# Transposing u by DMA instead of on TensorE, from the third batch on

## The chip, the cores and the metric

One core of one Trainium2 chip runs the whole program. The metric is device time in microseconds (us) of that core. A single core has no second die to compare with. A run's device time is about 2 us longer than the span of its trace.

Short names: PE is TensorE doing matmuls, PEld TensorE loading weights (it overlaps PE), DVE VectorE, ACT ScalarE, POOL GpSimd, SP SyncE; SPq is SyncE's queue of DMA issues. L946 is line 946 of the kernel that was profiled, so the same statement has other line numbers in other versions: ch1 is L988 before and L1008 after, ch2 is L1008 before and L1028 after.

## The reference, cut to what matters

A linear attention with a norm is followed by an MLP block over 8 batches of 576 tokens and 512 features:

```python
kv  = einsum('bhsd,bhse->bhde', k, v)
out = einsum('bhsd,bhde->bhse', q, kv)
x   = out / rms(out) * g_norm                 # then heads are joined: (8, 576, 512)
tok = einsum('ts,bsd->btd', w_tok, alpha1 * x + beta1)
u   = x + lam * tok
a2  = alpha2 * u + beta2
ch  = maximum(a2 @ w_ch1, 0) @ w_ch2          # 512 -> 2048 -> 512
return u + lam * ch
```

`u` is made with tokens on the partitions, and `a2 @ w_ch1` contracts over the features, so u has to be transposed before the first MLP matmul (ch1). alpha2 and beta2 belong to features, so after the transposition they are one value per partition.

## The kernel before

The kernel is a list scheduler written in Python: every operation is entered with its possible engines, an estimated cost on each and the tiles that it reads and writes. The scheduler simulates the engines, picks an engine and a place in program order for each operation, and semaphore waits are then put between the engines. Each engine runs its own list strictly in order.

The part that the change replaces is `ut(b)`, for one batch:

```python
def ut(b, pri):
    nc4 = 5 if b % 2 else 4            # odd batches carry the 64-row tails of two batches
    n = 128 * nc4
    def group(djs):
        t = P.ptile(1)                 # a PSUM bank
        for i, dj in enumerate(djs):
            for c in range(nc4):
                P.op({"PE": 0.056}, lambda e, _, ...: e.transpose(
                    bt(i)[:, 128 * c:128 * c + 128], ub[:, c, 128 * dj:128 * dj + 128], identb[:]),
                    r=[..., ("ub", c)], w=[t], kind="T", keep=1, after=[("a2t", dj)])
        for i, dj in enumerate(djs):
            # ACT: activation(Identity, scale=alpha2 column, bias=beta2 column)
            # DVE: tensor_scalar(mult, add) with the same columns; PSUM -> a2t
            ...
    # one group for each of the four blocks of 128 features
```

ub holds u in bf16, tokens on partitions. a2t holds the scaled transpose, [128, 4, 640] bf16, in a single buffer: it cannot be filled for batch b + 1 before the ch1 matmuls of batch b are done with it. In between lie the ch2 matmuls of batch b and the token mixing of batch b + 1.

## Time and profile before

| quantity | before |
|---|---|
| time, median of 4 runs | 373.49 us (372.63 to 374.49) |
| span of the trace | 371.9 us |
| PE busy | 361.9 us, 97% |
| transposes of u on PE | 144, of which 108 from the third batch on |
| PE idle from 103 to 331 us | none |

The first part of the profile page gives busy time, share of the span and number of instructions of each engine:

```profile
PE 361.9 (97%) x2279; PEld 224.1 (60%) x2279; DVE 224.4 (60%) x393; ACT 176.6 (47%) x304; POOL 119.8 (32%) x113
```

TensorE is the bound. Busy time by stretches shows it again (columns: stretch, its length, then busy time and count on PE, PEld, DVE, ACT and POOL, granted clock, share of the DMA engines, GB/s):

```profile
147.00:169.00 22.00, 22.00 (x132) 12.15 (x130) 11.84 (x21) 4.63 (x8) 5.58 (x4) 1.00 0.24 81
189.00:215.00 26.00, 26.00 (x153) 14.70 (x152) 15.58 (x27) 5.61 (x11) 8.50 (x6) 1.00 0.10 38
```

In the steady part PE has no gap, the clock is full, and from 147 us on the DMA engines are mostly idle, because all inputs have been loaded. From 103 to 131 us their share is still 0.52. Work taken from PE here shortens the run one for one, as long as nothing new makes PE wait.

The transposes, and the instructions that evict them, by source line (duration in ns, minimum/median/maximum):

```profile
L946 PE MATMUL ps<-identb,ub x144: 219/219/233, 31.1 to 319.3; 128*128 128x128 bf16 x144
L954 ACT ACTIVATE a2t<-ps,cols x11: 769/876/884, 78.7 to 320.3; 128x640 bf16<-128x640 bf16 x7, 128x512 bf16<-128x512 bf16 x4
```

The 219 ns are one transpose from end to end. They are pipelined, and the chain that ended last shows what they cost in a row (columns: start, time, what):

```profile
317.36 0.89 PE ps L946 x16
318.26 1.08 PE ps L1008 x5
...
331.00 17.39 PE ps L988 x128
348.38 17.28 PE ps L1008 x80
```

Sixteen transposes take 0.89 us, 56 ns each. The two last lines are the MLP of the last batch: its ch1 starts at 331.00 us. The end of the run, from SyncE's timeline (start, length):

```profile
367.13 1.11 SPq L1028 DMA_DIRECT2D out_dram<-xtl  x2
```

### The profile page before, as it was taken

Reading aid. Unit: us, or ns where it says so; the run is one execution under the profiler, and the core shown is the slowest. Engines: PE = TensorE matmul, PEld = TensorE weight load, DVE = VectorE, ACT = ScalarE, POOL = GpSimd, SP = SyncE. Lnnn points to the kernel's source line nnn. Section 1 sums busy time; section 2 is a strip of 40 time slices with the busy share of each in tenths; the row PEclk is TensorE's granted clock in tenths of the full one; section 3 lists DMA queues with packets and bytes.
Section 4 is the critical chain, followed back from the end, with each engine's and each line's share of the span. In section 5 each row is a group of like instructions: output and inputs, shape, how many; then the busy total and the mean of one; then the engine's idle time right before and its main releaser. Section 6 shows DMA issues by size and latency. Waiting matters only on the chain.

```text
span 371.9 us, 5712 instructions
## 1 busy us (share of the span) xinstructions
PE 361.9 (97%) x2279; PEld 224.1 (60%) x2279; DVE 224.4 (60%) x393; ACT 176.6 (47%) x304; POOL 119.8 (32%) x113
## 2 busy tenths in 40 slices
PE   8999999999999999999999999999999999999993
PEld 2787574678766564558855665557755544557541
DVE  3779579993985786738944682738453794410132
ACT  3778775676864276116821376116621273116300
POOL 3654014530353560045502571046502650130000
PEclk9999999999999999999999999999999999999998
DMA  6999999998658119111000110011000210020021
GB/s 179 365 372 386 289 381 303 375 368 250 204 156 269 59 56 335 35 56 58 0 2 28 58 57 2 0 56 58 2 0 28 86 28 0 31 85 2 0 86 56
DMA packets 47798, 48.01 MB, mean 129 GB/s; under 512 B 14096, under 2 KB 38680, under 8 KB 47772
## 3 DMA queue, kind: packets, MB, share of 16 engines
q1 hardware_dynamic: 47520, 47.47, 38.2%
q8 instruction: 18, 0.29, 0.3%
q10 hardware_dynamic: 252, 0.18, 0.1%
q14 instruction: 8, 0.07, 0.1%
HBM read 38.20 MB, written 9.44 MB: 128 GB/s over the span
## 4 chain that ended last, share of the span: by engine, by line
PE 86%; DMA 6%; DVE 4%; ACT 2%; SPq 1%; issue 0%
PE ps L988 33%; PE ps L1008 31%; PE ps L916 10%; DMA st<-in_v_dram 6%; PE ps L591 4%; PE ps L609 3%; PE ps L946 2%; DVE rt L692 1%; DVE yn L690 1%; PE ps L741 1%; ACT w L422 1%; PE ps L1095 1%; DVE small L679 0%; ACT wt L422 0%; PE ps L814 0%; ACT vr L422 0%
## 5 line engine op out<-in xcount | busy, mean ns | idle before, releaser
L988 PE MATMUL ps<-a2t,w 128*128 128x320 bf16 (+1 forms) x768 | 142.3, 329 | 1.7 <-DVE ht L974 0.7
L1008 PE MATMUL ps<-w,ht 128*128 128x512 bf16 x576 | 139.6, 381 | 0.0
L988 PEld LDWEIGHTS ps<-a2t,w 128*128 128x128 bf16 x768 | 73.3, 98 | 44.3 <-DVE ht L974 1.6
L1008 PEld LDWEIGHTS ps<-w,ht 128*128 128x128 bf16 x576 | 54.8, 98 | 59.2
L973 ACT ACTIVATE ht<-ps 128x640 bf16<-128x640 f32 (+1 forms) x103 | 67.2, 653 | 45.0 <-PE ps L988 44.2
L1021 POOL TENSOR_TENSOR xm<-xm,lc 128x512 f32<-128x512 f32 x28 | 37.4, 1335 | 129.5 <-DVE lc L1016 129.5
L1016 DVE TENSOR_TENSOR lc<-ps,lam_bc 128x512 f32<-128x512 f32 x36 | 24.9, 691 | 66.5 <-PE ps L1008 65.8
L695 POOL TENSOR_TENSOR xm<-yn,g_bc 128x512 f32<-128x512 f32 x28 | 43.2, 1543 | 38.3 <-DVE yn L690 37.2
L677 ACT ACTIVATE sq<-ps 128x512 f32<-128x512 f32 (+1 forms) x35 | 20.5, 593 | 47.9 <-PE ps L591 47.6
L924 DVE TENSOR_TENSOR xm<-ps,xm 128x512 f32<-128x512 f32 x28 | 19.2, 690 | 31.0 <-PE ps L916 29.8
L916 PE MATMUL ps<-rt,wt 128*128 128x512 bf16 x140 | 37.3, 381 | 0.0
L591 PE MATMUL ps<-kvc,qt 128*128 128x128 f32 x112 | 32.6, 386 | 0.0
L591 PE MATMUL ps<-identr,qr 128*128 128x128 f32 x112 | 31.6, 375 | 0.4 <-DVE yn L690 0.4
L609 PE MATMUL ps<-vr,kr 128*128 128x128 f32 (+1 forms) x112 | 30.9, 370 | 0.0
L679 DVE TENSOR_REDUCE small<-sq 128x8 f32<-128x512 f32 (+1 forms) x35 | 23.4, 672 | 7.7 <-ACT sq L677 7.2
L692 DVE TENSOR_TENSOR rt<-yn,ge 128x512 bf16<-128x512 f32 x26 | 25.1, 971 | 0.5
L954 ACT ACTIVATE a2t<-ps,cols 128x640 bf16<-128x640 bf16 (+1 forms) x11 | 8.9, 842 | 32.8 <-PE ps L946 32.8
L690 DVE TENSOR_TENSOR yn<-ps,small 128x512 f32<-128x512 f32 (+1 forms) x35 | 23.9, 685 | 0.7
L591 PEld LDWEIGHTS ps<-kvc,qt 128*128 128x128 f32 x112 | 22.1, 199 | 2.3
L916 PEld LDWEIGHTS ps<-rt,wt 128*128 128x128 bf16 x140 | 13.6, 98 | 15.3
L591 PEld LDWEIGHTS ps<-identr,qr 128*128 128x128 f32 x112 | 22.0, 201 | 1.2 <-DVE yn L690 0.7
L609 PEld LDWEIGHTS ps<-vr,kr 128*128 128x128 f32 x112 | 21.7, 200 | 0.3
(147 smaller groups left out, 386.5 us busy)
## 6 DMA issues: line engine op xcount, KB each, us to landing
st<-in_moe_w_ch_dram SPq DMA_DIRECT2D x8, 1024.0 KB, 10.9
out_dram<-xm SPq DMA_DIRECT2D x32, 256.0 KB, 2.3
st<-in_q_dram SPq DMA_DIRECT2D x7, 1024.0 KB, 6.3
st<-in_k_dram SPq DMA_DIRECT2D x7, 1024.0 KB, 8.5
st<-in_v_dram SPq DMA_DIRECT2D x7, 1024.0 KB, 11.7
ht<-in_moe_w_tok_dram SPq DMA_DIRECT2D x2, 576.0 KB, 8.1
kvft<-in_k_dram SPq DMA_DIRECT2D x8, 128.0 KB, 7.3
kvft<-in_v_dram SPq DMA_DIRECT2D x8, 128.0 KB, 5.4
```

Of the source, the lines that this page charges most:

```text
L591: P.op(F, lambda e, _: e.matmul(t.flat()[:, 128 * pr:128 * pr + 128], a(), m(), start=True, stop=True), r=r, w=[t], kind="F", **kw)
L609: return e.matmul(o, a, m, start=(c == 0), stop=(c == 4))
L679: P.op({"DVE": dve_us(512)}, lambda e, _: e.tensor_reduce(out=small[rows, s4], in_=sq[rows, s2], axis=AX.X, op=ALU.add), r=[("sq", s2)], w ...
L690: P.op({"DVE": dve_us(512)}, lambda e, _: e.tensor_tensor(out=hview(yn[rows, s3, :]), in0=hview(t.flat(rows)), in1=bc, op=ALU.mult), r=[t, ...
L692: P.op({"DVE": dve_us(512), "POOL": pool_us(512)}, lambda e, _: e.tensor_tensor(out=rto, in0=yn[rows, s3, :], in1=ge1[rows, :], op=ALU.mul ...
L695: P.op({"POOL": pool_us(512)}, lambda e, _: e.tensor_tensor(out=hview(x), in0=hview(yn[rows, s3, :]), in1=g_bc[rows, None, :].to_broadcast ...
L916: return e.matmul(t.flat(), wt[:, sc, col:col + 128], rt[:, sc, :] if sc < 4 else rtt[:], start=(sc == 0), stop=(sc == 4))
L973: return e.activation(dst, src(), ACT.Relu)
L988: return e.matmul(o, w1[:, dj, 128 * fj:128 * fj + 128], m, start=(dj == 0), stop=(dj == 3))
L1008: P.op({"PE": 0.216}, lambda e, _: e.matmul(t.flat(), ht[:, fj, 128 * c:128 * c + 128], w2[:, fj, :], start=(fj == 0), stop=(fj == 15)), r ...
L1016: o = P.op({"DVE": dve_us(512)}, lambda e, _: e.tensor_tensor(out=lc[:], in0=t.flat(), in1=lam_bc[:], op=ALU.mult), r=[t, "lam"], w=["lc"] ...
L1021: lambda e, _: e.tensor_tensor(out=x, in0=x, in1=lc[:], op=ALU.add),
```

## The change

The intent is to take the transposes off the bounding engine. From the third batch on, each chunk of 128 tokens of ub goes through a transposing DMA on SyncE's queue straight into a2t, and alpha2 and beta2 are applied in place in SBUF. The scaling is free to run on ACT or DVE; no PSUM is used.

```diff
-                    if ye == e and e != "POOL" and y not in o.raw:
-                        continue
@@ the kernel
+        XB = 2
@@ def ut(b, pri)
+            if b >= XB:
+                before = set(o for dj in range(4) for o in P.readers.get(("a2t", dj), ()))
+                before.update(o for dj in range(4) for o in P.lastw.get(("a2t", dj), ()))
+                for c in range(nc4):
+                    o = P.op({"SP": 0.5}, lambda e, _, c=c: e.dma_start(
+                        a2t[:, :, 128 * c:128 * c + 128], ub[:, c, :], transpose=True),
+                        r=[("ub", c)] if c < 4 else [("ubt", 0), ("ubt", 1)], w=[("a2r", c)],
+                        dma_us=0.6, pri=pri)
+                    o.deps.update(before)
+                for dj in range(4):
+                    ... # in place: a2t = a2t * alpha2 + beta2, on ACT or DVE
+                    P.op({"ACT": act_us(n, 2), "DVE": dve_us(n, 4)}, g,
+                         r=["cols"] + [("a2r", c) for c in range(nc4)], w=[("a2t", dj)],
+                         pri=pri - 5, port=True)
+                return
```

The first hunk makes an engine also wait on itself before it overwrites what it has read.

More of the change, by code (lines that the diff above doesn't have):

```diff
@@ L937, in ut, with g @@
             n = 128 * nc4
+            if b >= XB:
[8 more added lines that the diff above has]
+                for dj in range(4):
+                    def g(e, m, dj=dj):
+                        if m == "ACT":
+                            return e.activation(a2t[:, dj, 0:n], a2t[:, dj, 0:n], ACT.Identity,
+                                                scale=cols[:, dj:dj + 1], bias=cols[:, 4 + dj:5 + dj])
+                        return e.tensor_scalar(out=a2t[:, dj, 0:n], in0=a2t[:, dj, 0:n],
+                                               scalar1=cols[:, dj:dj + 1], scalar2=cols[:, 4 + dj:5 + dj],
+                                               op0=ALU.mult, op1=ALU.add)
+                    P.op({"ACT": act_us(n, 2), "DVE": dve_us(n, 4)}, g,
+                         r=["cols"] + [("a2r", c) for c in range(nc4)], w=[("a2t", dj)],
+                         pri=pri - 5, port=True)
+                return
             def group(djs):
```

## The prediction

> **What bounds the kernel now.** TensorE. The page's first part gives PE 97% of the 371.9 us span (DVE 60%, ACT 47%, POOL 32%). In the busy time by stretches PE has no gap from 103 to 331 us; the granted clock is 1.00. The chain that ended last is 86% PE, the transposes of u (L946) 2.0%. The DMA is full until about 85 us; from 147 us its share is 4 to 24%.
>
> **What the change removes.** From the third batch on, 108 of 144 transposes (three batches of 20, three of 16). One shows as 219 ns, but they are pipelined: 16 of them advance PE by 0.89 us in the chain (317.36 to 318.26), 14 by 0.80 us, so 56 ns each. 108 x 56 ns = 6.0 us, all on the critical path as PE has no gaps there: 373.7 - 6.0 = 367.7 us, 1.6%. Also gone are 24 evictions from PSUM (ACT 876 ns, DVE 545 ns median), worth nothing as neither engine limits.
>
> **What it adds.** 27 transposing DMAs of 128x512 bf16 (128 KB) on SyncE, and 24 in-place scalings in SBUF, mostly on VectorE, estimated at 0.3 to 0.5 us, off the path.
>
> **Does the transpose arrive in time?** a2t has one buffer, so the window lies between the u casts and the next batch's first ch1 matmul. Timeline: the last casts start at 114.8, 154.1, 196.4, 238.4, 279.2, 317.9; ch1 at 130.7, 168.8, 215.1, 253.0, 296.4, 330.8. That leaves 12.5 to 18 us after the last cast, 18 to 24 after the first, less about 1 us as ch1 comes earlier. SyncE only stores after 147 us.
>
> One chunk: plain stores of 128 KB and 256 KB land 2.3 us after issue, issue taking 0.33 to 0.6 us. The Trainium skill, "DMA: Bandwidth & Descriptors", section "Latency and other measured facts", gives 261 GB/s for a DMA transpose: estimate 0.5 us for 128 KB, so landing in about 3 us, all landed 5 us after the last cast, no PE wait. "VectorE: DVE Perf Modes", section "The three transpose paths", gives 1309 ns for 128x128: four per chunk serially would be 5.2 us, and five chunks 26 us from the first cast (149.1 to about 177), a stall of some 8 us in each of three odd batches. I take the first as likelier. No run here shows either yet.
>
> **Other effects.** Same-engine write-after-read orders become semaphore waits. A wait on its own previous result costs DVE about 0.1 us (starts 0.71 instead of 0.61 us apart); few are adjacent. I allow 0.3 us, in the start-up up to 66 us, where the chain runs through DVE. Otherwise the first 110 us should be unchanged. The third batch's DMAs meet loads in flight near 107 to 117 us, with 15 us of slack.
>
> **Prediction.** 368.0 us, 80% range 366.4 to 375. Faster by over 2% (below 366.2): 0.06; within 2%: 0.84; slower by over 2%: 0.10. The removed PE work bounds the gain under 2%.
>
> **What would show it.** L946 falls from 144 to 36. PE stays gapless after 103 us; ch1 waits for neither DVE a2t nor the DMA. Transposes land within 2 to 4 us; SyncE issues each in 0.5 to 2 us. Wrong if PE waits for a2t before each ch1, or landing exceeds 5 us.
>
> **What would make it wrong.** Transposes served serially at 5 us or more per chunk; a SyncE issue of several us; a late DMA blocking VectorE in program order, so that PSUM evictions stall PE; or the re-made list schedule moving other work onto the path.

## More of the kernel before

The scheduler prefers to alternate "F" matmuls (float32r, attention) with others, and at the end SyncE waits for every DMA of the program, one wait for each:

```python
rank = (fresh, (o.kind == "F") == (last_kind == "F"))
...
for o in self.sequence:
    if o.lat is not None:              # o is a DMA
        nc.sync.wait_ge(*val[o.idx])
```

## The result

Ratios here are the mean time of one kernel's runs over that of the other's runs of the same rounds, so they are not quite the ratio of the medians.

| | before | after |
|---|---|---|
| time, median of 4 runs | 373.49 us | 368.49 us (368.14 to 368.84) |
| ratio, 95% interval | | 0.9865 [0.9838, 0.9892] |
| span of the trace | 371.9 us | 366.1 us |
| first ch1 matmul of the second batch | 79.65 us | 79.62 us |
| first ch1 matmul of the last batch | 330.83 us | 323.84 us |
| from the one to the other ("the stretch") | 251.19 us | 244.22 us |
| end of the last DMA issue to the end of the span | 3.6 us | 4.9 us |

The run is 5.0 us shorter, 1.35%, against a predicted 368.0 us. The stretch in the table is useful because it hardly varies: everything in it is bound by PE. (Its lengths are taken from unrounded starts.) It is read from PE's timeline, where the matmul itself starts; the chain above lists the same place 0.17 us later. The start-up before it, bound by loads, moves from run to run (in the profiled runs other than experiment 7 the second batch's ch1 starts at 78.7 to 80.0 us), which is also why the two profiled runs differ by 5.8 us and the medians by 5.0.

The profile after, first part of the page:

```profile
PE 355.1 (97%) x2142; PEld 218.4 (60%) x2171; DVE 223.4 (61%) x394; ACT 175.3 (48%) x301; POOL 121.2 (33%) x115
```

PE is 6.8 us less busy and still 97% of a shorter span; it bounds as before. (The count of matmuls fell by 137 instead of 108 because some records are missing from the trace; the count of weight loads fell by exactly 108.) The instructions that use a2t now:

```profile
L941 SPq DMA_TRANSPOSE a2t<-ub x27: 1188/1224/2206, 112.4 to 312.5; - x27
L951 DVE TENSOR_SCALAR a2t<-a2t,cols x19: 401/434/1359, 125.6 to 316.2; 128x512 bf16<-128x512 bf16 x10, 128x640 bf16<-128x640 bf16 x9
L949 ACT ACTIVATE a2t<-a2t,cols x5: 802/920/921, 123.4 to 315.0; 128x640 bf16<-128x640 bf16 x3, 128x512 bf16<-128x512 bf16 x2
...
DMA to landing us min/median/max: 2.4/2.5/6.7
```

SyncE spends 1.2 us on the issue of a transpose of 128x512, which lands 2.5 us after its start (medians). The third batch's transposes meet loads: from 112.4 to 121.7 us the DMA engines are full, and its four transposes land 6.7, 5.2, 3.2 and 3.0 us after their starts. The last batch in time order, from the timelines of SP, DVE, ACT and PE:

```profile
307.09 6.64 SPq L941 DMA_TRANSPOSE a2t<-ub  x5
314.98 0.92 ACT L949 ACTIVATE a2t<-a2t,cols 128x640 bf16<-128x640 bf16 x1 [9.55 <-DMA a2t<-ub]
314.98 1.64 DVE L951 TENSOR_SCALAR a2t<-a2t,cols 128x640 bf16<-128x640 bf16 x3 [0.60 <-DMA a2t<-ub]
323.84 17.55 PE L1008 MATMUL ps<-a2t,w 128*128 128x320 bf16 x128
```

The scaled transpose is complete at 316.6 us, 7.2 us before ch1 asks for it. In the third to seventh batch this slack is 1.8, 8.2, 13.9, 8.4 and 11.7 us. The third is the tightest: its transposes have landed by 123.4 us, but DVE comes to the scaling in its list only at 125.58 us and is done at 127.58 us:

```profile
125.58 2.00 DVE L951 TENSOR_SCALAR a2t<-a2t,cols 128x512 bf16<-128x512 bf16 x3
129.34 1.68 PE L1008 MATMUL ps<-a2t,w 128*128 128x512 bf16 x7
```

PE's waits from 81 to 362 us hold nothing of a2t:

```profile
PE ps L1008 <- ACT ht L993: 0.4, 1, 0.4
PE ps L1008 <- ACT qt L420: 0.4, 1, 0.4
```

And the end, from SyncE's timeline:

```profile
360.14 1.12 SPq L1048 DMA_DIRECT2D out_dram<-xtl  x2
```

The last issue ends at 361.26 us and the span at 366.1 us. So two sizes differ from the prediction: the stretch shrank by 6.97 us where 6.0 was forecast, and the end grew by 1.2 us, which was not forecast at all.

The theory that the experiments test has four parts. First, the gain is PE time alone. Second, a transpose is worth more than 56 ns because some of them stood next to float32r matmuls. Third, the end grew because SyncE executes 27 more waits there, one after the other. Fourth, the transposes have several us to spare, but only because the DMA engines are idle at that time. The rivals are that the gain comes from the PSUM evictions that ACT and DVE no longer do, that the end grew for another reason, and that the arrival was nearly too late. (The slacks above already limit the fourth part: the third batch's transposes came in time with the DMA engines full, and had 1.8 us to spare, not several.)

### The profile page after: what moved, and what is told of

Its sections match the earlier page's. It is cut to its first block, busy times and chain, and to the rows that moved or that the text cites. A ratio compares the mean times of both kernels' runs of the same rounds, so it can differ in the third digit from the quotient of the medians.

```text
span 366.1 us, 5530 instructions
## 1 busy us (share of the span) xinstructions
PE 355.1 (97%) x2142; PEld 218.4 (60%) x2171; DVE 223.4 (61%) x394; ACT 175.3 (48%) x301; POOL 121.2 (33%) x115
## 4 chain that ended last, share of the span: by engine, by line
PE 90%; DVE 6%; ACT 1%; issue 1%; POOL 0%
PE ps L1008 35%; PE ps L1028 31%; PE ps L915 9%; PE ps L590 4%; PE ps L1115 4%; PE ps L608 2%; PE ps L864 1%; DVE rt L691 1%; DVE yn L689 1%; PE ps L835 1%; PE ps L740 1%; PE ps L1128 1%; DVE lc L1036 1%; PE ps L767 1%; DVE small L678 0%
## 5 line engine op out<-in xcount | busy, mean ns | idle before, releaser
L1028 PE MATMUL ps<-w,ht 128*128 128x512 bf16 x562 | 137.7, 382 | 0.5
L1028 PEld LDWEIGHTS ps<-w,ht 128*128 128x128 bf16 x576 | 55.0, 98 | 60.5
L915 PE MATMUL ps<-rt,wt 128*128 128x512 bf16 x134 | 36.1, 381 | 0.2
L691 DVE TENSOR_TENSOR rt<-yn,ge 128x512 bf16<-128x512 f32 x24 | 23.8, 1001 | 0.4
L949 ACT ACTIVATE a2t<-a2t,cols 128x640 bf16<-128x640 bf16 (+1 forms) x5 | 4.4, 875 | 40.2 <-DMA a2t<-ub 40.2
## 6 DMA issues: line engine op xcount, KB each, us to landing
st<-in_v_dram SPq DMA_DIRECT2D x7, 1024.0 KB, 10.7
```

The costliest lines, as they stand in the source:

```text
L691: P.op({"DVE": dve_us(512), "POOL": pool_us(512)}, lambda e, _: e.tensor_tensor(out=rto, in0=yn[rows, s3, :], in1=ge1[rows, :], op=ALU.mul ...
L915: return e.matmul(t.flat(), wt[:, sc, col:col + 128], rt[:, sc, :] if sc < 4 else rtt[:], start=(sc == 0), stop=(sc == 4))
L1028: P.op({"PE": 0.216}, lambda e, _: e.matmul(t.flat(), ht[:, fj, 128 * c:128 * c + 128], w2[:, fj, :], start=(fj == 0), stop=(fj == 15)), r ...
```

## The experiments

All twelve kernels gave a correct result. Their runs shared runs of the kernel before on the same chip, whose median was 374.03, 374.17 and 373.89 us in the three sets.

### 1. The transposes put back on PE as dead work

```diff
                     o.deps.update(before)
+                for dj in range(4):
+                    t = P.ptile(1)
+                    for c in range(nc4):
+                        P.op({"PE": 0.056}, lambda e, _, c=c, dj=dj, t=t: e.transpose(
+                            ..., ub[:, c, 128 * dj:128 * dj + 128], identb[:]),
+                            r=[...], w=[t], pri=pri, kind="T", keep=1, after=[("a2t", dj)])
```

> The kernel after, with the 108 TensorE transposes put back as dead work: into PSUM, with no eviction and no reader. Theory (the gain is TensorE time): the first ch1 matmul of the last batch moves back from 324.0 to about 331 us, and the time is about 368.5 + 7.0 = 375.5 us, slower than before by the longer end. Rival (the gain is the 24 PSUM evictions that ScalarE and VectorE no longer do, or the PSUM banks): the time stays near 368.5 us.

Measured: 375.09 us, ratio to before 1.0037 [1.0011, 1.0063]. The stretch is 251.75 us, where before has 251.19 and after 244.22. The chain that ended last:

```profile
331.51 17.39 PE ps L1016 x128
```

So the whole gain goes away when PE has its transposes back, although ACT and DVE still do no PSUM evictions. The dead transposes take their PSUM banks again too, so this run does not separate PE time from banks; but before the change PE never stood idle from 103 to 331 us, so no missing bank held it up there. The gain is PE time. The kernel is even 1.1 us slower than before by median, mainly by its longer end: from the last issue to the end of the span it takes 4.9 us, as the kernel after does.

### 2, 3 and 4. The waits at the end

```diff
             for o in self.sequence:
-                if o.lat is not None:
+                if o.lat is not None and not any(o in s.deps for s in o.succ):
                     nc.sync.wait_ge(*val[o.idx])
```

This keeps the waits for DMAs that no instruction waits for, the 12 last output stores. Every other DMA has been waited for by its reader. It is applied to the kernel after (e2) and to the kernel before (e3). In e4 the loop of the kernel after stands twice.

> The kernel after, where SyncE's waits at the very end cover only DMAs that no instruction waits for (some 12 output stores) instead of all 136. Theory (the end is SyncE's string of waits, about 44 ns each from 1.18 us for 27 more): the stretch from the last issue to the end falls from 4.84 us to about 2 us, where the landing of the last store (2.4 us after issue) sets it; time about 366.0 us. Rival (the longer end comes from more semaphores or from the clock that fell to half): the stretch stays at 4.8 us and the time at 368.5 us.

> The kernel before with the same cut of its 109 waits at the end. Theory: its last stretch falls from 3.66 us to about 2 us, time about 372.0 us, so that the difference to the kernel after with the same cut is the whole TensorE gain, 6 to 7 us. Rival: no change, 373.5 us.

> The kernel after with its 136 waits at the end issued twice. Theory (44 ns each, run one after the other): last stretch 4.84 + 136 x 0.044 = 10.8 us, time about 374.4 us. Rival (waits that are already met cost nothing): 368.5 us.

| kernel | waits at the end | last issue to end of span | time | ratio to before |
|---|---|---|---|---|
| before | 109 | 3.6 us | 374.03 us | |
| after | 136 | 4.9 us | 368.49 us | 0.9865 |
| e4, twice | 272 | 10.7 us | 373.71 us | 0.9995 [0.9971, 1.0018] |
| e2, after with few | 12 | 2.1 us | 365.24 us | 0.9762 [0.9737, 0.9786] |
| e3, before with few | 12 | 2.1 us | 372.44 us | 0.9957 [0.9935, 0.9979] |

(The row "after" is of the first measurement, with its own runs of before.) In SyncE's timeline the last issue of e2 and of e4:

```profile
360.01 1.12 SPq L1048 DMA_DIRECT2D out_dram<-xtl  x2
```

```profile
360.43 1.12 SPq L1051 DMA_DIRECT2D out_dram<-xtl  x2
```

The spans end at 363.2 and 372.2 us. The waits themselves are in the traces, two to an instruction; in before, after and e4 (duration in ns, then first and last start in us):

```profile
L405 SPq EVENT_SEMAPHORE  x55: 17/28/28, 368.3 to 371.6; - x55
L403 SPq EVENT_SEMAPHORE  x68: 28/28/28, 361.3 to 365.8; - x68
L406 SPq EVENT_SEMAPHORE  x136: 27/28/1746, 361.6 to 371.9; - x136
```

Waits that were met long ago are executed one after the other, an instruction each 61 ns, so about 30 ns for a wait. From 109 to 136 waits the end grows by 1.2 us: 0.8 us for 13 more instructions, and 0.4 us mostly in one pause near the end of the row, which e4 has at the same place; its cause stays open. From 136 to 272 waits it grows by 5.8 us: 4.1 us for 68 more instructions, and 1.7 us because the first one of e4 lasts 1.75 us, until the last store has landed, which in after happens while the row runs. So the 44 ns per wait of the expectations was too high, and it was luck that the 10.8 us expected of e4 met 10.7. The part of the theory about the end holds, and cutting the waits removes more than the change had added. With the waits cut on both sides the stretches are unchanged (244.22 and 251.19 us), and the difference of the medians, 372.44 - 365.24 = 7.2 us, is the change without its longer end.

### 5, 6 and 9. How late may the transposes be?

In the last batch alone, one (e5) or two (e6) transposing DMAs into unused memory are put ahead of each real one:

```diff
                 for c in range(nc4):
+                    for nm in 'q' if b == 7 else ():          # e6: 'qk'
+                        i = held[nm, b]
+                        y = P.op({"SP": 0.5}, lambda e, _, c=c, i=i: e.dma_start(
+                            st[:, i] ..., ub[:, c, :], transpose=True), ...)
                     o = P.op({"SP": 0.5}, lambda e, _, c=c: e.dma_start(
```

> The kernel after, in the last batch alone one extra transposing DMA into unused memory ahead of each of the five real ones. Theory (SyncE gives one transpose per 1.22 us, scaling ended at 316.6 us, ch1 started at 323.8 us, so 7.2 us of slack): scaling ends about 6.1 us later, at 322.7 us, still in time; PE does not wait; time 368.5 + 0.2 (five more waits at the end) = 368.7 us. Rival (the transposes already arrive just in time): about 6 us slower, 374.5 us.

> As the last, with two extra ones ahead of each real one. Theory: scaling ends about 12.2 us later, at 328.8 us, so PE waits about 5 us before the last batch's ch1; time 368.5 + 5.0 + 0.4 = 373.9 us. Rival (DMA transposes overlap, and the issue is not what sets the pace): no wait, about 369 us.

Measured: e5 372.69 us, ratio 0.9961 [0.9926, 0.9996]; e6 375.20 us, ratio 1.0028 [0.9991, 1.0065]. The expectation for e6 (373.9) is roughly met, that for e5 (368.7) clearly missed: 4 us were lost although the scaling was in time. From the timelines of e5:

```profile
321.77 1.52 DVE L962 TENSOR_SCALAR a2t<-a2t,cols 128x640 bf16<-128x640 bf16 x4 [7.01 <-DMA a2t<-ub]
323.21 0.68 DVE L1047 TENSOR_TENSOR lc<-ps,lam_bc 128x512 f32<-128x512 f32 x1
323.95 5.27 PE L1039 MATMUL ps<-w,ht 128*128 128x512 bf16 x16 [3.01 <-DVE lc L1047]
```

The scaling ended at 323.3 us, as expected. But it stood in DVE's list ahead of the eviction of a ch2 tile (L1047). DVE waited 7.0 us for the DMA with that eviction behind it, no PSUM bank came free, and PE stood still for 3.0 us in the middle of ch2, not at ch1. The deadline of the transposes is thus not ch1's start but the place in DVE's list at which the scheduler put the scaling. In e6 the scheduler happened to put it one eviction later, and PE waited where the theory said, for a2t:

```profile
329.13 6.08 PE L1019 MATMUL ps<-a2t,w 128*128 128x320 bf16 x27 [4.92 <-ACT a2t L960]
```

Both stalls cost more than their length, because the clock fell. Busy time by stretches of e5, columns as before:

```profile
321.00:323.00 2.00, 0.00 (x0) 0.00 (x0) 1.23 (x4) 0.00 (x0) 0.00 (x0) 1.00 0.41 145
323.00:325.00 2.00, 1.05 (x3) 0.44 (x4) 0.89 (x2) 0.00 (x0) 1.03 (x1) 0.72 0.00 0
325.00:327.00 2.00, 2.00 (x6) 0.70 (x5) 0.69 (x1) 0.00 (x0) 1.13 (x2) 0.50 0.34 131
```

After the 3 us of idleness PE ran at a granted clock of 0.51 for 3.5 us (323.9 to 327.4 us), so it lost another 1.7 us. Together with the 3.0 us that is 4.7 us, and the stretch of e5 is 249.05 us, 4.83 more than that of after. The Trainium skill, "TensorE: Matmul & The Clock Gate", section "Why this matters for your kernels", advises to have no PE-idle gaps over about 3 us between bursts of matmuls; this trace agrees, but experiment 7 shows that shorter gaps can be enough.

That reading of e5 can be tested. In e9 the scheduler is told what the traces show SyncE to need for a transpose, so that it places the scaling later; nothing else is changed:

```diff
-                        y = P.op({"SP": 0.5}, ...        and    o = P.op({"SP": 0.5}, ...
+                        y = P.op({"SP": 1.27}, ...       and    o = P.op({"SP": 1.27}, ...
```

> As the doubled transposes (372.7 us), but the list scheduler is told 1.27 us of SyncE time per transpose instead of 0.5, so that it places the last batch's scaling on VectorE after two more evictions of ch2. Theory (the 3.0 us wait of PE in that run was VectorE standing in program order at the scaling, with an eviction behind it, not the transposes being late for ch1): no PE wait before ch1, time 368.5 + 0.2 to 0.5 = about 369 us. Rival (ten transposes arrive too late however the engines are ordered): still 372 to 373 us.

Measured: 368.56 us, ratio 0.9862 [0.9844, 0.9880], the same as after, with ten transposes in the last batch instead of five. The scaling is as late as in e5, but PE does not wait:

```profile
321.55 2.49 DVE L962 TENSOR_SCALAR a2t<-a2t,cols 128x640 bf16<-128x640 bf16 x4
324.21 0.69 DVE L1047 TENSOR_TENSOR lc<-ps,lam_bc 128x512 f32<-128x512 f32 x1 [0.17 <-PE ps L1039]
```

```profile
324.01 9.26 PE L1019 MATMUL ps<-a2t,w 128*128 128x320 bf16 x67
```

It is the cost estimate that lost 4 us in e5, not the DMA.

### 7. From the second batch on

```diff
-        XB = 2
+        XB = 1
```

> The kernel after with XB = 1: the second batch is transposed by DMA too. Theory (the window must be free of loads: the DMA share is 1.0 from 60 to 81 us and plain loads of 128 KB land 4 to 10 us after issue there, while only some 3 us lie between the last cast near 76.5 us and ch1 at 79.7 us): the 20 transposes saved (1.3 us) are lost to a PE wait of 4 to 10 us, part of it made up later only by the loads; time 371 to 376 us. Rival (transposes pass the loads): 367.2 us.

Measured: 377.63 us, ratio 1.0070 [1.0019, 1.0122]; the expected range ended at 376. The theory is right in kind: the second batch's transposes are issued from 73.9 to 85.3 us into a queue full of loads. In this run a transpose lands up to 9.7 us after issue, and ch1 of the second batch starts late:

```profile
89.38 1.51 DVE L951 TENSOR_SCALAR a2t<-a2t,cols 128x640 bf16<-128x640 bf16 x4
89.88 0.45 PE L1008 MATMUL ps<-a2t,w 128*128 128x320 bf16 x1 [1.30 <-DVE a2t L951]
```

It starts at 89.88 instead of 79.6 us. The wait before it is booked as 1.3 us only, because PE and DVE had other delayed work in between; and the clock had halved, from 80.88 to 94.53 us. Three of the stretches that show it:

```profile
78.00:80.00 2.00, 1.03 (x9) 0.74 (x7) 1.97 (x4) 1.97 (x4) 1.19 (x1) 1.00 1.08 375
80.00:82.00 2.00, 1.35 (x7) 1.21 (x7) 1.61 (x2) 1.06 (x2) 0.77 (x2) 0.72 1.80 321
84.00:86.00 2.00, 2.00 (x11) 2.00 (x11) 0.78 (x2) 0.78 (x2) 0.00 (x0) 0.50 1.22 304
```

In the 3.41 us before the clock fell PE was busy for 1.98 us, and none of its gaps there was longer than 0.7 us. I had left the clock out, which is the likely reason for the larger loss; its part was not measured by itself. PE was busy for 11.8 us of the 13.7 us at half clock, so by my estimate at most 5.9 us of the delay are the clock's.

The loads are not the only thing that differs here. In the kernel after, the second batch's last cast ends at 77.6 us and its ch1 starts at 79.6 us, 2.0 us later; the last batch, with the DMA engines far from full (share 0.41), needs 4.2 us from the end of its last cast (312.46 us) to the end of the scaling. So the second batch would probably be late without loads too, while the third batch has 14 us between the same two points (115.2 and 129.3 us) and arrives in time among loads. The two causes, loads and too short a window, were not separated. The change is not a better transposition as such: it works where the window is long enough.

### 8. Only the last three batches

```diff
-        XB = 2
+        XB = 5
```

> The kernel after with XB = 5: only the last three batches (56 of the 108 transposes) by DMA. Theory (65 ns of TensorE time per transpose removed): PE starts the last batch's ch1 at about 331.0 - 3.6 = 327.4 us, with 13 waits fewer at the end than after (0.6 us); time about 368.5 + 3.4 - 0.6 = 371.3 us. Rival (the gain is made in one place, such as the loaded third batch, or by another schedule): near 368.5 or near 373.5 us.

Measured: 370.79 us, ratio 0.9913 [0.9880, 0.9945]; the last ch1 starts at 327.39 us. The stretch is 247.89 us, 3.30 less than before for 56 transposes, 59 ns each. The gain is spread over the batches. The remaining 52, of the third to fifth batch, are then worth 3.67 us, 71 ns each. Experiment 11 explains the difference: of 22 transposes that follow a float32r matmul in the trace of before, 17 are in those three batches and 5 in the last three.

### 10. The old wait rule

```diff
+                    if ye == e and e != "POOL" and y not in o.raw:
+                        continue
                     if ye == e and e == "PE":
```

> The kernel after with the two removed lines of the wait rule put back; its program differs from after by four waits of VectorE on itself in the start-up and nothing else. Theory (the rule costs nothing that counts): 368.5 us within 0.5. Rival (the wait rule costs time, or the start-up gains by it): different by over 1 us.

Measured: 367.95 us, ratio 0.9843 [0.9822, 0.9864], overlapping that of after; stretch 244.23 us. The profiled runs reach the second batch's ch1 at 79.67 and 79.62 us, so no cost of the rule is seen. The medians, 0.5 us apart, are too noisy to rule out the 0.3 us that the prediction allowed for it.

### 11. What a transpose costs beside a float32r matmul

The starts of PE instructions in a row, from PE's timeline of the kernel before; L591 are float32r matmuls, L946 transposes:

```profile
153.50 0.23 PE L946 MATMUL ps<-identb,ub 128*128 128x128 bf16 x1
153.55 0.30 PE L591 MATMUL ps<-kvc,qtt 128*128 128x128 f32 x1
153.69 0.23 PE L946 MATMUL ps<-identb,ub 128*128 128x128 bf16 x1
153.73 0.30 PE L591 MATMUL ps<-kvc,qtt 128*128 128x128 f32 x1
```

And the same matmuls after the change, now beside wide matmuls of ch2 (L1028):

```profile
151.91 0.39 PE L1028 MATMUL ps<-w,ht 128*128 128x512 bf16 x1
151.96 0.41 PE L590 MATMUL ps<-kvc,qtt 128*128 128x128 f32 x1
152.21 0.39 PE L1028 MATMUL ps<-w,ht 128*128 128x512 bf16 x1
```

A pair of transpose and float32r matmul takes 0.19 us, a pair of wide matmul and float32r matmul 0.29 to 0.30. A transpose alone takes 0.056 us and a wide matmul alone 0.216. So the float32r matmul adds about 0.074 us beside a wide one and 0.134 beside a transpose. A likely reason is its weight load of 200 ns, which a wide matmul covers and a transpose does not. The trace of before has 22 such neighbours (a transpose right after a float32r matmul) from the third batch on. To test it, the kernel before is kept, and only the class by which the scheduler alternates is changed:

```diff
-                            w=[t], pri=pri, kind="T", keep=1, after=[("a2t", dj)])
+                            w=[t], pri=pri, kind="T" if b < 2 else "F", keep=1, after=[("a2t", dj)])
```

In its program none of the 108 transposes has a float32r neighbour; each stands between wide matmuls.

> The kernel before, with the 108 transposes kept on TensorE but put by the scheduler between wide matmuls instead of next to float32r matmuls (22 such neighbours before, none here). Theory (a transpose costs 56 ns, and one beside a float32r matmul hides less of that one's 200 ns weight load: the pair takes 190 ns, while the float32r one beside a wide matmul adds only 74): 22 x 60 ns = 1.3 us less PE time, last ch1 starts at 331.0 - 1.3 = 329.7 us, time 1.3 us below before. Rival (the 7.0 us of the change against my 6.0 comes from something else): no change against before.

Measured: 372.62 us, ratio to before 0.9975 [0.9953, 0.9996]. The stretch is 250.19 us, 1.00 us less than before. Of the 0.97 us by which the change gained more than forecast, this accounts for all within the accuracy of the argument; my own estimate of 1.3 us was a little high.

### 12. A version to beat both

```diff
  the end waits of e2, and
-                    o = P.op({"SP": 0.5}, ...
+                    o = P.op({"SP": 1.27}, ...
-                            w=[t], pri=pri, kind="T", keep=1, after=[("a2t", dj)])
+                            w=[t], pri=pri, kind="F" if b == 1 else "T", keep=1, after=[("a2t", dj)])
```

> A version to beat both: after with the end waits cut to the DMAs that nothing waits for, the scheduler told 1.27 us of SyncE per transpose, and the second batch's 20 TensorE transposes kept away from float32r matmuls. Theory: 365.2 us as the end-wait cut alone, perhaps 0.3 us less by the transposes; 365.0 us. Rival (a re-made schedule gives it back): 366 us or more.

Measured: 366.84 us, ratio 0.9816 [0.9793, 0.9838]. That is better than both kernels, but 1.6 us worse than e2 by median, so the two additions lose. The stretch is 247.01 us, 2.8 us longer than in e2. The loss is early; the stretch from 81 to 103 us in the kernel after (the first line) and in e12:

```profile
81.00:103.00 22.00, 21.43 (x178) 18.21 (x180) 14.84 (x27) 16.85 (x30) 6.03 (x4) 1.00 0.78 247
```

```profile
81.00:103.00 22.00, 19.91 (x170) 17.17 (x168) 17.53 (x29) 17.39 (x31) 5.08 (x4) 1.00 0.76 243
```

PE is idle for 1.5 us more there. Experiment 9 tells which of the two additions did it: it has the 1.27 us too, and there the third batch's ch1 starts 49.44 us after the second's, as in e2 (49.43 us); in e12 it takes 52.53 us. So the 1.27 us do not lose this time by themselves; the other class of the second batch's transposes does, alone or together with them. That it made the scheduler lay out this part worse is likely, but was not looked into. **The best version is e2: the change with the end waits cut, 365.24 us, 2.4% below before.**

## Why the prediction was right

- **What bounds.** "TensorE ... PE has no gap from 103 to 331 us": right, and experiment 1 shows that the gain is PE time and nothing else.
- **"16 of them advance PE by 0.89 us ..., so 56 ns each. 108 x 56 ns = 6.0 us".** Right in mechanism, too small in size: the stretch shrank by 6.97 us, 65 ns for each transpose. The 56 ns were read where transposes stand in a row. Twenty-two of them stood beside float32r matmuls, and parting them gained 1.00 us without any DMA (experiment 11).
- **Landing in time.** The issue was put at 0.5 to 2 us and measures 1.2; the landing was put at 2 to 4 us and measures 2.5 by median. The 5.2 us per chunk of the pessimistic case, an estimate from the 1309 ns of "VectorE: DVE Perf Modes", did not come true as a rule. But two transposes of the third batch landed after 6.7 and 5.2 us, over the 5 us that the prediction had named as a sign of being wrong, and that batch's last one landed 8 us after the last cast where 5 us were forecast. PE never waited for a2t all the same. The slack was read as 12.5 to 18 us after the last cast; what was left of it was 1.8 us in the third batch and 7.2 us in the last.
- **Same-engine waits.** 0.3 us were allowed; by the program the rule adds four waits, and no cost was seen, though 0.3 us is within the noise (experiment 10).
- **What was not forecast.** 27 more DMAs mean 27 more waits at the program's end, 1.2 us (experiments 2 to 4). No step of the prediction asked what is done once per DMA. The omission and the gain that was put 1 us too small nearly cancelled, so that 368.0 came out next to 368.49; the number was better than its parts.
- **A hazard named and nearly met.** "A late DMA blocking VectorE in program order, so that PSUM evictions stall PE" did not happen in the change as given, but exactly that happened in experiment 5, when the scaled transpose came 6.7 us later (323.3 instead of 316.6 us).

## What to carry to other kernels

A move of work from the bounding engine to an idle path is worth its time on the bounding engine in its real neighbourhood, not that of a clean run of the same instruction; and what a mover brings once per piece, here a wait at the end for each DMA, belongs in the sum. Where engines run in program order, the deadline of a late input is where its consumer stands in the list, with everything queued behind it: give the scheduler the issue time that the trace shows. Move transposes to the DMA only where the time from the last input to the first use is longer than they take under the DMA load of that stage: here 14 us among loads were enough, and 2 us were not.

## What the Trainium skill lacked or had wrong

- "DMA: Bandwidth & Descriptors", "Latency and other measured facts", gives 261 GB/s for a DMA transpose whose middle dimension is not contiguous. Here the issue set the pace: in experiment 5 SyncE started one transpose of 128x512 bf16 (128 KB) each 1.31 us, about 100 GB/s. The section gives no issue time for such a transpose, which is what limited it; elsewhere the page has cycles for it only in a comparison of trn3 with "previous generations".
- "VectorE: DVE Perf Modes", "The three transpose paths", sets 390 ns (TensorE) against 1309 ns (DMA) for 128x128. Neither is a cost in a stream: on TensorE one takes 219 ns, but 56 ns in a row and 65 ns on average as removed here; by DMA four of them together land 2.5 us after issue and occupy SyncE for 1.2 us.
- "TensorE: Matmul & The Clock Gate", "What's actually happening", puts the fall of the clock after an idle window of about 3.4 us. A gap of 3.0 us (3.5 us without a weight load) was enough in experiment 5, and then 3.5 us ran at a clock of 0.51. In experiment 7 it fell after 3.41 us in which PE was busy for 1.98 us, with no gap over 0.7 us; and at the end of a run it fell 2.0 us after the last matmul in the kernel after, 4.3 us after it in the kernel before.
- No page that I read has the cost of a wait that is already met: about 30 ns on SyncE in the row at the end (one instruction, which holds two waits, each 61 ns).
- No page that I read has what a float32r matmul adds by its neighbour: 74 ns beside a wide bf16 matmul, about 134 ns beside a 128-column transpose.
